# Attention reads and a mixture of experts on one core: x transposed by transfers inside SBUF, weights converted to fp16 on their way in

## The chip, the core and the metric

The kernel runs on one core of a Trainium2 chip. The metric is the device time of one execution in microseconds (us); less is better. Five engines work side by side, each through its own instruction queue and in the order in which the kernel recorded its instructions: TensorE (PE, matrix products; its weight loads are listed as PEld), VectorE (DVE), ScalarE (ACT), GpSimd (POOL) and SyncE (SP, which only issues transfers). Transfers (DMA) are issued from an engine's queue and run on 16 DMA engines beside it. TensorE and the transfers meet in SBUF; TensorE's products land in the eight banks of PSUM, from which DVE or ACT must copy ("evict") them.

## The reference

Stage one is attention between `x` (8 batches, 8 heads, 512 rows, 64 columns) and a small `state` (32 rows per head), both ways; stage two sends the 4352 resulting rows of 512 numbers through 8 experts, all of them, weighted by a routing matrix P that is normalised by rows and columns eight times (Sinkhorn).

```python
scores  = scale * x @ state.T;  a  = softmax(scores);   xread = a @ state
scores2 = scale * state @ x.T;  a2 = softmax(scores2);  sread = a2 @ x
x = concat([xread, sread], axis=2)          # rows of all heads side by side
P = exp(x @ w_gate - max)
for _ in range(8):                          # Sinkhorn
    P /= P.sum(1);  P /= P.sum(0);  P *= N / E
for e in range(E):
    out += P[:, e:e+1] * (relu(x @ w1[e]) @ w2[e])
```

`w1[e]` is 512 x 1024 and `w2[e]` is 1024 x 512, both fp32 in HBM: 4 MB per expert. `x` is 8 MB.

## The kernel before, in words

**Two stages of code.** Lines 353 to 858 build a list of operations `ops`, and `issue(ops)` (line 48) records them in an order of its own. The code calls this the plan of the first stage: attention for all batches, the gate and Sinkhorn, the whole of expert 0, and the first layer of expert 1 for two blocks. From line 884 on, a plain loop over experts 1 to 7 and nine blocks of rows (eight blocks of 512 rows, one per batch, and one of 256) records the second stage: `layer2` of one block interleaved with `layer1` of the next and `project` of the one after.

**The plan.** Each operation has engines with a busy time and a latency (the pairs in braces, in us), operations that it comes after, and buffers that it takes or uses. `issue` always records the operation that can start earliest by these numbers; among equals the lowest rank decides. Ranks are due times: `due_x(u)` (line 354) for half-batch `u` of attention, `due_e(bi)` (line 355) for block `bi` of expert 0, `due_1` (line 356) for expert 1. The plan only sets the order in each queue. On the chip every engine takes its queue strictly in that order and waits by semaphores.

**Attention, per batch `b`.** Two loads of 512 KB each (`load`, line 443, SP's queue, two buffers `x_st`) bring four heads each. A cast to fp16 into `x_nat` (line 448) runs on DVE and ACT for batch 0 and on POOL for batches 1 to 7, four instructions per half. Then `turn` (line 510) transposes `x_nat` on TensorE: four 128 x 128 transposes into one PSUM bank for each of four head pairs, 16 per batch, 128 in all. `keep` (line 515) evicts each bank into `xT` on DVE or ACT, 32 evictions in all. Each half-batch `q` then needs two head pairs of `xT`: scores `psA` and `psB` (lines 534 and 541), maxima, exponentials and sums on DVE and ACT, one normalisation `a` on POOL (`normA`, line 577), transposes back (lines 597 and 601), and `su_ps` (line 619), which reads `x_nat` again. The result is `aT` for the rows and `xsT` for the state side.

**Weights.** For experts 0 and 1, `weights_ops` (line 463) splits the 4 MB into eight loads of 512 KB on SP's queue into three staging buffers `wst`, each followed by a cast to fp16 on ACT or DVE (`cast`, line 478), to `w1h` and `w2h`. For experts 2 to 7, `load_w` (line 159) is a generator that the main loop advances now and then (`step`, line 875): eight loads on SP's queue (lines 170 and 175), each cast two turns later by ACT (line 181), and then eight subtractions on DVE (line 196) that build `T` from `w2h`. `w1h` and `w2h` have two buffers each, so expert `e+1` is loaded while `e` runs.

**Expert work on TensorE.** V products from `w1h` (`v_ps`, line 722, and line 237 in the second stage), first layer `hps` (line 746; line 252), second layer `yps` (line 781) for expert 0, and in the second stage seven products per block with a trick that needs sums on DVE (line 298; sums in lines 277 to 280). DVE adds the weighted result into `acc` (line 312). Experts 1 to 7 need P from Sinkhorn before their first addition; Sinkhorn (lines 669 to 703) runs as one chain between DVE and TensorE, whose matmul is `csb_ps` (line 701), and starts when the last gate product is there.

Of the kernel before, what the change touches and what calls it, by code (L numbers as in the profile page):

```python
# [87 lines left out]
def kernel(  # L88
# [64 lines left out]

    mwst = ctx.enter_context(tc.tile_pool(name="moe_wst", bufs=3))
    mw = ctx.enter_context(tc.tile_pool(name="moe_w", bufs=2))
# [3 lines left out]
    def load_w(e, engines):  # L159
# [3 lines left out]
        w16[e] = (w1h, w2h)  # L163
        casts = []
        n = NKC + NFB // 2
        for k in range(n + 2):
            if k < n:
                if k < NKC:
                    st = mwst.tile([128, F], FP32, name="w1st", tag="wst")
                    nc.sync.dma_start(out=st, in_=w1r[e, :, k, :])  # L170
                    casts.append((w1h[:, k, :], st))
                else:
                    g = k - NKC
                    st = mwst.tile([128, 2, Dm], FP32, name="w2st", tag="wst")
                    nc.sync.dma_start(out=st, in_=w2r[e, :, ds(g * 2, 2), :])
                    casts.append((w2h[:, ds(g * 2, 2), :], st))
            if k >= 2:
                dst, src = casts[k - 2]
                eng = engines[(k - 2) % len(engines)]
                if eng is nc.scalar:  # L180
                    nc.scalar.copy(out=dst, in_=src)  # L181
                else:
                    eng.tensor_copy(out=dst, in_=src)
            yield
# [19 lines left out]
    actx = ExitStack()  # L204
    axs = actx.enter_context(tc.tile_pool(name="attn_xs", bufs=2))
    axp = actx.enter_context(tc.tile_pool(name="attn_x", bufs=3))
# [146 lines left out]
    ops = []  # L353
    due_x = lambda u: 10.0 + 5.54 * u
    due_e = lambda bi: 25.1 + 13.7 * bi
    due_1 = 150.0
    rings = {"bank": Ring(8)}
# [28 lines left out]
    def dma(rank, kb, emit, after=(), takes=()):  # L386
        return op(rank, {"DMA": (kb / 330.0, kb / 330.0 + 2.2)}, lambda _: emit(), after, takes)


# [46 lines left out]

    xn = [slot(axp, 3, [128, NSC, H, D], FP16, "x_nat") for _ in range(B)]
    x_ready = []
    for b in range(B):
        for g in range(2):  # L440
            st = slot(axs, 2, [128, H // 2, NSC * D], FP32, "x_st")

            def load(b=b, g=g, st=st):
                nc.sync.dma_start(
                    out=st.tile,
                    in_=x[b, ds(g * 4, 4), :, :].rearrange("h (p sc) d -> p h (sc d)", sc=NSC))

            def cast(eng, b=b, g=g, st=st):
                src = st.tile.rearrange("p h (sc d) -> p sc h d", sc=NSC)
                for sc in range(NSC):  # L450
                    copy(eng, xn[b].tile[:, sc, ds(g * 4, 4), :], src[:, sc])

            d = dma((0 if b < 1 else due_x(2 * b - 2), b, 0), 512, load, takes=[st])
            on = {"DVE": (0.90, 1.10), "ACT": (1.35, 1.50)} if b == 0 else {"POOL": (1.65, 1.80)}
            x_ready.append(op((0, 3) if b == 0 else (due_x(2 * b - 2),), on, cast, [d] + x_ready[2 * b:],
                              [xn[b]] if g == 0 else [], [st] + ([xn[b]] if g else [])))
# [5 lines left out]

    def weights_ops(e, rank, on):
        w1 = slot(mw, 2, [128, NKC, F], FP16, "w1h")
        w2 = slot(mw, 2, [128, NFB, Dm], FP16, "w2h")
        wslots[e] = (w1, w2)
        for k in range(NKC + NFB // 2):
            first = k < NKC
            st = slot(mwst, 3, [128, F], FP32, "wst")

            def load(k=k, st=st):
                if k < NKC:
                    nc.sync.dma_start(out=st.tile, in_=w1r[e, :, k, :])
                else:
                    nc.sync.dma_start(out=st.tile.rearrange("p (a b) -> p a b", a=2),
                                      in_=w2r[e, :, ds((k - NKC) * 2, 2), :])

            def cast(eng, k=k, st=st):
                if k < NKC:
                    copy(eng, w1.tile[:, k, :], st.tile)  # L480
                else:
                    copy(eng, w2.tile[:, ds((k - NKC) * 2, 2), :],
                         st.tile.rearrange("p (a b) -> p a b", a=2))

            d = dma(rank + (k,), 512, load, [w_ready.get((e, k - 1))] if k == 1 else [], [st])
            takes = [w1] if k == 0 else [w2] if k == NKC else []
            before = [w_ready[e, 0]] if 0 < k < NKC else [w_ready[e, NKC]] if k > NKC else []
            w_ready[e, k] = op(rank + (k,), on, cast, [d] + before, takes, [st])

    def w1_ready(e):  # L490
        return [w_ready[e, k] for k in range(NKC)]

    def w2_ready(e):
        return [w_ready[e, k] for k in range(NKC, NKC + NFB // 2)]

    weights_ops(0, (3.0, 4), {"ACT": (0.95, 1.10), "DVE": (0.75, 0.95)})
    weights_ops(1, (due_1 - 30.0, 0), {"ACT": (0.95, 1.10), "DVE": (0.75, 0.95)})


# [4 lines left out]
    for b in range(B):  # L504
        xT = slot(axt, 2, [128, NP, S], FP16, "xT")
        xt_ready = {}
        for hp in range(NP):
            ps = psum([128, S], FP16, "xT_ps")

            def turn(_, b=b, hp=hp, ps=ps):  # L510
                for sc in range(NSC):
                    nc.tensor.transpose(ps.tile[:, ds(sc * 128, 128)],
                                        xn[b].tile[:, sc, ds(2 * hp, 2), :], identh)

            def keep(eng, hp=hp, ps=ps, xT=xT):
# [5 lines left out]
                              [t] + ([xt_ready[0]] if hp else []),  # L521
                              [] if hp else [xT], [ps] + ([xT] if hp else []))
        for q in range(NQ):
            r = lambda n, b=b, q=q: (due_x(2 * b + q) + 0.1 * 5.54 * n,)
            psA = psum([128, NSC, 4, Ns], FP32, "psA")
# [93 lines left out]
            def read(_, b=b, q=q, ETs=ETs, su=su):  # L619
                for par in range(2):  # L620
                    for sc in range(NSC):
                        nc.tensor.matmul(su.tile[:, par].rearrange("p i n -> p (i n)"),
                                         xn[b].tile[:, sc, ds(2 * (2 * q + par), 2), :],
                                         ETs.tile[:, sc, ds(par * 64, 64)],
# [129 lines left out]
    for bi in range(len(blocks)):  # L754
# [6 lines left out]
        for fb in range(NFB):  # L761
# [8 lines left out]

            t = op((due_e(bi) + 0.05 * 13.7 * fb,), {"PE": (0.44, 0.62)}, mul, deps, [ps], held)
            h_ready.append(op((due_e(bi) + 0.05 * 13.7 * fb,), EVICT32, act, [t], [h], [ps]))
            hT.append(h)
        for tk in range(tn // 128):
            yps = psum([128, Dm], FP32, "yps")
            last = None
            for half in range(2):
                def mul(_, tk=tk, half=half, yps=yps, hT=hT):
                    w2h = wslots[0][1].tile
                    for fb in range(half * NJ, half * NJ + NJ):  # L780
# [3 lines left out]
                fbs = range(half * NJ, half * NJ + NJ)  # L784
                last = op((due_e(bi) + 13.7 * (0.4 + 0.075 * (2 * tk + half)),), {"PE": (0.87, 1.04)}, mul,
                          [h_ready[fb] for fb in fbs] + w2_ready(0)[2 * half:2 * half + 2] + [last],
                          [] if half else [yps], [hT[fb] for fb in fbs] + ([yps] if half else []))
# [3 lines left out]

            op((due_e(bi) + 13.7 * (0.4 + 0.075 * (2 * tk + 1)),), EVICT32, keep, [last], [], [yps])

# [141 lines left out]
```

## Time and profile before

| what | value |
|---|---|
| median of 3 runs | 794.11 us (793.38 to 795.03) |
| the profiled execution | 794.67 us |
| its span, first to last instruction | 792.9 us |
| mean granted TensorE clock | 0.995 of full |
| busy: PE, DVE, ACT, POOL | 764.5, 648.8, 566.7, 39.5 us |
| bytes read from HBM, written | 42.48 MB, 8.91 MB |
| last `csb_ps` of Sinkhorn, end of its chain | 161.89 us, about 164.2 us |
| first product of the second stage's loop (line 298) | 165.46 us |

How to read it: a busy engine is one with an instruction under way. Matmuls overlap each other in the pipeline, so TensorE's busy time says whether it idles, not how fast it works; what one instruction costs is read from the distance between starts. A "group" gathers instructions of one line, engine and shape, with the mean duration of one and the idle time of the engine ahead of them. A "wait" says which engine stood still for which producer. The timeline merges equal instructions that follow each other: start, time from the first start to the last end, count.

### The profile page before, as it was taken

The numbers are of one execution on the slowest core, as the hardware profiler recorded it, in microseconds if no ns is written. First come the engines' busy times: TensorE is split into PE (matmuls) and PEld (weight loads), VectorE is DVE, ScalarE is ACT, GpSimd is POOL, SyncE is SP. The second block draws the span as 40 slices with busy tenths as digits, with TensorE's granted clock in tenths as the row PEclk, the third lists the DMA queues.
The fourth block names the chain that finished last, engine by engine and source line by source line (L and its number), as shares of the span: only waits on it lengthen the run. The fifth ranks groups of instructions, "written<-read, shape, count | busy, mean of one in ns | idle before, by whom it ended". The sixth has DMA issues, their size and how long they took to land.

```text
span 792.9 us, 16564 instructions
## 1 busy us (share of the span) xinstructions
PE 764.5 (96%) x6593; PEld 514.2 (65%) x6593; DVE 648.8 (82%) x1603; ACT 566.7 (71%) x1072; POOL 39.5 (5%) x80
## 2 busy tenths in 40 slices
PE   4899999989999999999999999999999999999996
PEld 3455554556667666766667666766667766767675
DVE  7898877787898888978788888978788888978885
ACT  5787776568977688577866688578866688576662
POOL 1543210000000000000000000000000000000000
PEclk9999999999999999999999999999999999999999
DMA  8874000002400033001410033001400030002233
GB/s 280 288 253 138 1 2 1 1 1 64 125 28 1 1 104 111 1 2 54 129 33 2 1 107 107 1 2 54 133 28 2 1 107 28 1 24 97 95 107 134
DMA packets 29535, 52.46 MB, mean 66 GB/s; under 512 B 4625, under 2 KB 12817, under 8 KB 29457
## 3 DMA queue, kind: packets, MB, share of 16 engines
q1 hardware_dynamic: 28368, 51.14, 20.3%
q8 instruction: 51, 0.84, 0.4%
q10 hardware_dynamic: 1088, 0.26, 0.2%
q14 instruction: 28, 0.22, 0.1%
HBM read 42.48 MB, written 8.91 MB: 65 GB/s over the span
## 4 chain that ended last, share of the span: by engine, by line
PE 63%; DVE 4%; ACT 2%; issue 0%; DVEq 0%
PE hps L252 22%; PE Bseed L298 16%; PE E L298 11%; PE A L298 10%; PE v_ps L237 3%; DVE acc L312 2%; ACT Hm L271 2%; DVE sm L277 1%; ACT w2h L181 1%; DVE sm L280 0%; DVE Hm L278 0%; DVE T L196 0%; DVE sm L279 0%; ACT w1h L181 0%; DVE acc L320 0%
## 5 line engine op out<-in xcount | busy, mean ns | idle before, releaser
L271 ACT ACTIVATE Hm<-hps 128x512 f16<-128x512 f32 (+1 forms) x488 | 262.3, 575 | 149.8 <-PE hps L252 138.9
L298 PEld LDWEIGHTS <-Hm 128*128 128x128 f16 x1904 | 185.4, 98 | 74.4 <-issue 3.9
L252 PE MATMUL hps<-aT,V 128*128 128x512 f16 x864 | 230.5, 379 | 0.0
L312 DVE SCALAR_TENSOR_TENSOR acc<-Bseed,Pmat,acc 128x256 f32<-128x256 f32 x357 | 156.9, 479 | 57.1 <-PE Bseed L298 53.6
L298 PEld LDWEIGHTS <-sm 128*128 128x128 f16 x1428 | 134.4, 98 | 54.9 <-DVE sm L277 24.4
L298 PE MATMUL Bseed<-T,Hm 128*128 128x256 f16 x952 | 124.5, 273 | 2.7 <-DVE acc L312 2.5
L298 PE MATMUL A<-w2h,Hm 128*128 128x256 f16 x952 | 126.1, 273 | 0.5
L252 PEld LDWEIGHTS <-V 128*128 128x128 f16 x864 | 84.5, 98 | 44.4
L241 ACT CAST V<-v_ps 128x512 f16<-128x512 f32 x216 | 111.0, 608 | 0.0
L312 DVE SCALAR_TENSOR_TENSOR acc<-E,Pmat,acc 128x256 f32<-128x256 f32 x238 | 104.4, 478 | 5.4 <-PE E L298 1.0
L277 DVE TENSOR_TENSOR sm<-Hm 128x512 f16<-128x512 f16 (+1 forms) x122 | 49.9, 409 | 21.6 <-ACT Hm L271 20.8
L298 PE MATMUL E<-T,sm 128*128 128x256 f16 x476 | 64.4, 274 | 0.7
L781 PE MATMUL yps<-w2h,hT 128*128 128x512 f16 x272 | 64.6, 379 | 0.0
L312 DVE SCALAR_TENSOR_TENSOR acc<-A,Pmat,acc 128x256 f32<-128x256 f32 x119 | 52.4, 479 | 15.0 <-PE A L298 14.9
L298 PE MATMUL Bseed<-T,sm 128*128 128x256 f16 x476 | 62.3, 272 | 2.3 <-ACT Bseed L323 2.3
L298 PE MATMUL E<-w2h,sm 128*128 128x256 f16 x476 | 62.3, 273 | 0.0
L278 DVE TENSOR_TENSOR Hm<-Hm 128x512 f16<-128x512 f16 (+1 forms) x122 | 50.0, 410 | 4.2
L280 DVE TENSOR_TENSOR sm<-Hm,sm 128x512 f16<-128x512 f16 (+1 forms) x122 | 50.0, 410 | 4.2
L279 DVE TENSOR_TENSOR sm<-sm,Hm 128x512 f16<-128x512 f16 (+1 forms) x122 | 49.1, 403 | 0.0
L323 ACT COPY Bseed<-A 128x512 f32<-128x512 f32 (+1 forms) x63 | 34.7, 552 | 18.7 <-PE A L298 15.6
L781 PEld LDWEIGHTS <-hT 128*128 128x128 f16 x272 | 24.8, 98 | 27.5 <-issue 2.6
L746 PE MATMUL hps<-aT,V 128*128 128x512 f16 x160 | 41.1, 389 | 0.4
(114 smaller groups left out, 626.1 us busy)
## 6 DMA issues: line engine op xcount, KB each, us to landing
w1st<-in_moe_w_dram SPq DMA_DIRECT2D x24, 512.0 KB, 3.6
w2st<-in_moe_w_dram SPq DMA_DIRECT2D x24, 512.0 KB, 3.6
x_st<-in_x_dram SPq DMA_DIRECT2D x16, 512.0 KB, 5.1
wst<-in_moe_w_dram SPq DMA_DIRECT2D x16, 512.0 KB, 6.1
out_dram<-acc SPq DMA_DIRECT2D x32, 256.0 KB, 3.1
out_dram<-acc SPq DMA_DIRECT2D x8, 64.0 KB, 1.7
st_st<-in_state_dram ACTq DMA_DIRECT2D x4, 64.0 KB, 3.2
st_st<-in_state_dram SPq DMA_DIRECT2D x4, 64.0 KB, 3.0
```

The costliest lines, as they stand in the source:

```text
L241: nc.scalar.copy(out=V[:, q, cols], in_=ps[q])
L252: nc.tensor.matmul(out, lhs, rhs, start=(k == 0), stop=(k == len(terms) - 1))
L271: nc.scalar.activation(out=Hm[:, i, j, :tn], in_=hps[:, :tn], func=AF.Relu)
L277: nc.vector.tensor_add(s1, a21, a22)
L278: nc.vector.tensor_sub(a21, a11, a21)
L279: nc.vector.tensor_sub(s2, s1, a11)
L280: nc.vector.tensor_sub(s4, a12, s2)
L298: nc.tensor.matmul(dst[:, c], lhs(j, c), rhs[:, j], start=first and c == 0 and j == 0, stop=(j == NJ - 1), skip_group_check=True)
L312: nc.vector.scalar_tensor_tensor(out=dst, in0=src[:, c], scalar=p[:, k], in1=dst, op0=ALU.mult, op1=ALU.add)
L323: nc.scalar.copy(out=Bb[:, :nk], in_=A[:, :nk])
L746: nc.tensor.matmul(ps.tile[:, :tn], lhs, rhs, start=(k == 0), stop=(k == len(terms) - 1))
L781: nc.tensor.matmul(yps.tile, hT[fb].tile[:, ds(tk * 128, 128)], w2h[:, fb, :], start=(fb == 0), stop=(fb == NFB - 1))
```

## The change

Three things change together; the arithmetic stays.

1. For batches 1 to 7 the 16 TensorE transposes and their four evictions per batch go. In their place two transfers per batch, issued from SP's queue, read half of `x_nat` ([128, 1024] fp16, 256 KB) and write it transposed, in blocks of 128 x 128, into `xT`, SBUF to SBUF. Batch 0 stays on TensorE. `x_nat` gets another layout for it, `x_st` gets three buffers instead of two.
2. All weights are loaded by GpSimd's queue in transfers of 1 MB of fp32, four per expert, which convert to fp16 on the way and write `w1h` and `w2h` directly. The staging buffers and all weight casts on ACT and DVE go. In `load_w` three empty turns follow the four transfers, so the subtractions for `T` come at turn 8 rather than at turn 11.
3. The due times change: `due_x` 10.0 + 5.77u, `due_e` 27.5 + 14.7bi, `due_1` 100, and expert 1's weights get rank 50 instead of 120. The plan is made anew with them, so the order in every queue of the first stage differs.

```diff
-        for k in range(n + 2):
...
+        for k in range(2):
+            nc.gpsimd.dma_start(out=w1h[:, ds(2 * k, 2)], in_=w1r[e, :, ds(2 * k, 2), :])
+            yield
+        for k in range(2):
+            nc.gpsimd.dma_start(out=w2h[:, ds(k * NJ, NJ)], in_=w2r[e, :, ds(k * NJ, NJ), :])
+            yield
+        for _ in range(3):
             yield
...
-    axs = actx.enter_context(tc.tile_pool(name="attn_xs", bufs=2))
+    axs = actx.enter_context(tc.tile_pool(name="attn_xs", bufs=3))
...
-    due_x = lambda u: 10.0 + 5.54 * u
-    due_e = lambda bi: 25.1 + 13.7 * bi
-    due_1 = 150.0
+    due_x = lambda u: 10.0 + 5.77 * u
+    due_e = lambda bi: 27.5 + 14.7 * bi
+    due_1 = 100.0
...
+    def dma16(rank, kb, emit, after=(), takes=(), uses=()):
+        asked = op(rank, {"POOL": (1.0, 1.0)}, lambda _: emit(), after, takes, uses)
+        return op(rank, {"DMA": (kb / 330.0, kb / 330.0 + 2.2)}, lambda _: None, [asked])
...
-    xn = [slot(axp, 3, [128, NSC, H, D], FP16, "x_nat") for _ in range(B)]
+    xn = [slot(axp, 3, [128, NP, NSC, 128], FP16, "x_nat") for _ in range(B)]
...
+            w_ready[e, k] = dma16(rank + (k,), 1024, load, [w_ready[e, k - 1]] if k % 2 else [],
+                                  [] if k % 2 else [w2 if k else w1], [w2 if k > 1 else w1] if k % 2 else [])
...
-    weights_ops(1, (due_1 - 30.0, 0), {"ACT": (0.95, 1.10), "DVE": (0.75, 0.95)})
+    weights_ops(1, (due_1 - 50.0, 0))
...
-        for hp in range(NP):
+        for hp in range(NP if b < 1 else 0):
...
+        for g in range(2 if b >= 1 else 0):
+            def turn(_, b=b, g=g, xT=xT):
+                nc.sync.dma_start_transpose(
+                    out=xT.tile[:, ds(2 * g, 2)].rearrange("p a (s t) -> p (a s) t", t=128),
+                    in_=xn[b].tile[:, ds(2 * g, 2)].rearrange("p a s c -> p (a s c)"))
+
+            t = op((due_x(2 * b + g) - 2.0, 0), {"SP": (1.6, 4.0)}, turn,
+                   [x_ready[2 * b + g]] + ([xt_ready[0]] if g else []), [] if g else [xT],
+                   [xn[b]] + ([xT] if g else []))
+            xt_ready[2 * g] = xt_ready[2 * g + 1] = t
```

## The prediction

> **What bounds the kernel now.** I read the busy time by stretches first, then the waits, then the timeline of TensorE.
>
> ```profile
> core 0: us, PE busy (x) PEld busy (x) DVE busy (x) ACT busy (x) POOL busy (x), PEclk, DMA share, GB/s
> 0.00:60.00 60.00, 45.56 (x466) 26.17 (x467) 49.55 (x117) 42.45 (x83) 23.68 (x55) 0.97 0.82 272
> 60.00:120.00 60.00, 59.68 (x577) 32.13 (x576) 49.18 (x117) 44.37 (x101) 15.82 (x25) 1.00 0.14 45
> 300.00:700.00 400.00, 399.29 (x3433) 282.29 (x3431) 330.25 (x822) 293.67 (x544) 0.00 (x0) 1.00 0.15 44
> ```
>
> Three stages. From 300 us on TensorE never idles (399.3 of 400), with ACT and DVE a fifth to a quarter idle. From 60 to 120 us the same. Only up to 60 us does TensorE stand idle, 14.4 us, while the transfers are 82% busy and DVE 83%.
>
> ```profile
> ACT Hm L271 <- PE hps L252: 138.9, 209, 1.9
> ```
>
> The longest wait of the run is ACT's for TensorE: in the second stage ACT has time to spare.
>
> ```profile
> 89.30 0.61 PE L512 MATMUL xT_ps<-identh,x_nat 128*128 128x128 f16 x8
> 89.74 1.03 PE L781 MATMUL yps<-w2h,hT 128*128 128x512 f16 x4
> ```
>
> Eight transposes of x hold TensorE from 89.30 to 89.74, where the next product starts: 0.44 us, 55 ns each (the group's mean of 241 ns counts overlap).
>
> ```profile
> 161.89 0.39 PE L701 MATMUL csb_ps<-cpart,ones 128*128 128x8 f32 x2
> 165.03 0.59 PE L871 MATMUL Bseed<-aT,identh 128*128 128x512 f16 x2 [1.01 <-ACT Hm L382]
> 165.46 1.04 PE L298 MATMUL A<-w2h,Hm 128*128 128x256 f16 x8
> ```
>
> The first stage ends for TensorE and for Sinkhorn together, at about 164 us; its last gate product was at 125.17 us, so Sinkhorn takes 39 us.
>
> **Part 1, transposes leave TensorE.** 7 batches x 16 x 55 ns = 6.2 us less on TensorE, which is full from 60 us to the end of the stage, so I count all of it. It shows at both ends: pricing the recorded matmuls of both orders by their distances in the trace (hps and yps 216 ns, psA 40, psB 166, v_ps 44, transposes 55, su_ps 30), the work ahead of the last gate falls from 100.7 to 93.4 us and the whole stage's from 136.7 to 130.5. Sinkhorn can thus start 7 us sooner, and TensorE runs dry 6 us sooner.
>
> The evictions go too:
>
> ```profile
> L376 ACT COPY xT<-xT_ps x18: 583/592/626, 12.8 to 110.7; 128x512 f16<-128x512 f16 x18
> L378 DVE COPY xT<-xT_ps x14: 361/415/425, 9.5 to 102.7; 128x512 f16<-128x512 f16 x14
> ```
>
> 18 x 0.59 + 14 x 0.41 = 16.1 us, less batch 0's four (2.0): 14 us of DVE and ACT, at nothing after 60 us, since TensorE covers them.
>
> What it adds: 14 transfers of 256 KB on SP's queue. The trace has none that transposes. Bounds from its packets: rows of 256 bytes (the state loads; 1088 packets on q10 took 0.2% of 16 engines' 792.9 us, 23 ns each) give 1024 x 23 / 16 = 1.5 us. Pieces of 32 bytes (the gate weights, 9 ns each in the packet records) give 8192 x 9 / 16 = 4.6 us. Between issue and landing some 2 to 3 us come on top (64 KB land after 1.7 us when stored, 3.0 to 3.2 when loaded).
>
> ```profile
> x_st<-in_x_dram SPq DMA_DIRECT2D x16, 512.0 KB, 5.1
> out_dram<-acc SPq DMA_DIRECT2D x32, 256.0 KB, 3.1
> wst<-in_moe_w_dram SPq DMA_DIRECT2D x16, 512.0 KB, 6.1
> ```
>
> So 3.1 us (same bytes, no transposing) to 4.6 + 3 = 7.6 us to landing; I take 4.5, near the rows of equal or double size, and keep both. Is that hidden? In the new order the first scores of batch 1 stand after 7.3 us of TensorE work, of batch 2 after 14.5, of batch 3 after 24.7, and two buffers `xT` let the transfers run one batch ahead; a batch lasts about 11 us. Two transfers at 3 to 4.6 us fit. Two that hold the stream more than 6.5 us each do not (rival B).
>
> SP's queue is in order: a transfer that waits for POOL's cast holds the x loads behind it. `x_st` has three buffers, so after the transfer of batch 1's first half three loads leave at once. Since weights no longer take turns in that queue, I cost this at nothing; if the cover goes, each batch arrives later by one wait, and rival B's sum holds.
>
> The timeline has 55 ns of TensorE's time for a 128 x 128 transpose among others; no row has one by transfer. The Trainium skill, "VectorE: DVE Perf Modes", section "The three transpose paths", speaks against the change: it lists 390 ns on TensorE and 1309 ns by transfer for one block. If that second figure were a price per block, a transfer of eight blocks would take 10.5 us (an estimate from that page) and rival B's sum would give 850 us.
>
> **Part 2, converting weight loads.** For experts 0 and 1, 16 casts (9 on ACT, 9.45 us; 7 on DVE, 6.27 us) go, all before 60 us, where DVE and ACT limit. In the second stage 48 casts of 1.04 us go from ACT: nothing from 300 us on, since ACT waits there anyway; between 165 and 260 us TensorE idles 4.8 of 95 us (90.23 busy), partly behind ACT and DVE: I take 1 us, bounds 0 and 3.
>
> Added: eight issues on POOL in the first stage. SP takes 0.37 to 0.5 us for an issue, POOL's normalisation 1.1 us; I take 1.0 each. In the new order five stand at the head of POOL's queue and end at about 1.8 + 5 = 7 us, long before the first normalisation.
>
> ```profile
> 15.14 1.43 POOL L378 CAST x_nat<-x_st 128x256 f16<-128x256 f32 x4 [13.33 <-DMA x_st<-in_x_dram]
> 16.53 1.10 POOL L578 TENSOR_TENSOR a<-eA,rA 128x512 f16<-128x512 f32 x1
> ```
>
> They matter only above (16 - 2) / 5 = 2.8 us each. What they do early is compete: 5 MB of weights are asked for by 7 us, beside x. In the trace 512 KB land every 1.3 us when the queue is full (weights at 11.04, 12.30, 13.63 us), 1 MB in 2.6 us. x of batch 0 landed at 7.89 and 9.46 us; with half the rate its second half lands 2.6 us later, and if 1 KB packets of x alternate with 4 KB packets of weights, about 9 us later. Against that stand three w1h casts ahead of the first hps at 24.74 us, two of ACT (1.05 each) and one or two of DVE (0.69), some 3 us, and a first transposing transfer that must wait behind a normalisation on POOL (about 1 us). Bounds -4 to +6 us, taken as 0.
>
> Conversion itself: as fast as plain loads (3 MB in 8 us) or as slow as 256-byte packets (178 GB/s, 17 us). w1h is whole at 15 to 25 us; the first v_ps now starts at 19.44 us. In the second stage 4 MB per expert, 628 us for seven experts, is little either way, and `T`'s subtractions, three turns earlier, come over 20 us after the request.
>
> **Part 3, due times.** Attention gets a little further ahead of expert 0, expert 1 moves ahead of expert 0's last blocks: the same work in another order, counted in the sums above, 0.
>
> **Sum, against the profiled execution of 794.67 us:** -6.2 (TensorE) - 1 (ACT, 165 to 260 us) + 0.7 (first waits on transposing transfers, of the bound 0 to 3) = -6.5, so 788.2. The median of the runs is 0.6 lower than the profiled execution; I give 788.
>
> **Rivals.**
>
> A. *The start gives it back.* x's first megabyte shares the transfers with 5 MB of weights, attention of batch 0 starts up to 6 us late, and TensorE, which has nothing else then, shifts as a whole. For: 82% busy transfers, TensorE idle 14 us up to 60 us. Against: fewer casts in just that stretch. 794.67 - 7.2 + 6 = 793.5.
>
> B. *Transposing transfers become the bound (slower).* First half ready at about 20 us; 14 in a row at t each; from the last scores (111.62 us) to the stage's end (164.2) the trace takes 52.6 us. End = 20 + 14t + 52.6: at 6.5 us it equals today's; at 7 it is 170.6 (801 us), at 8 184.6 (815 us). For: no row shows such a transfer, and one stream in SP's queue takes all 14. Against: the packets bound it at 4.6 us.
>
> C. *POOL is the bound (slower).* Issues above 2.8 us each delay normalisation and casts; at 4 us the first normalisation slips 6 us, and three later issues hold casts 3 us longer each, half of it hidden: 788.2 + 6 + 4.5 = 798.7. For: POOL serves one queue in order. Against: SP's issues take a tenth of that.
>
> D. *The start gains too:* DVE and ACT are relieved of 22 of 92 us before 60 us and TensorE's idle time shrinks by 4 us more: 783.
>
> That the change does not do what it says is excluded: the new order has 16 transposes of x on TensorE, not 128, and no weight cast.
>
> **How the numbers follow.** Forecast 0.50 (786 to 791), A 0.20, B 0.18, C 0.07, D 0.05. A difference under 0.2%, 1.6 us, cannot be told from none. Faster: 0.50 + 0.05 + a third of A (0.07) = 0.62. Same: 0.12 of A. Slower: 0.18 + 0.07 + 0.01 = 0.26. The range runs from D's far side, 782, to B at just over 7 us, 803; about 0.04 lies below and 0.16 above.
>
> **What would show it.** Right: the last csb_ps near 155 us, TensorE full from 50 us on, transposing transfers landing 4 to 5 us after issue, no psA that waits for xT after batch 1. Wrong: psA waiting for a transposing transfer in every batch (B), x of batch 0 landing after 12 us (A), POOL idle gaps at its issues (C), or a change beyond 300 us, where I expect none.

## The result, and the profile after

| | before | after |
|---|---|---|
| median | 793.64 us (793.22 to 795.03) | 795.16 us (793.96 to 798.05) |
| ratio, 95% interval | | 1.0023 [1.0014, 1.0031] |
| span of the profiled execution | 792.9 us | 793.9 us |
| first product `psA` of TensorE | 11.02 us | 23.83 us |
| first product of the second stage's loop | 165.46 us | 172.62 us |
| from there to the last product | 621.5 us | 615.3 us |

The change made the kernel slower by 0.23%, where I had forecast 0.8% faster. The table already says where: the loop over experts begins 7.2 us later and lasts 6.15 us less. The sum, 1.0 us, is the difference of the spans. Two large effects nearly cancel.

The same stretches as before the change, in the changed kernel:

```profile
core 0: us, PE busy (x) PEld busy (x) DVE busy (x) ACT busy (x) POOL busy (x), PEclk, DMA share, GB/s
0.00:60.00 60.00, 31.89 (x307) 17.86 (x308) 33.49 (x79) 22.77 (x52) 22.75 (x51) 0.97 0.91 187
60.00:120.00 60.00, 59.30 (x557) 30.04 (x556) 51.47 (x123) 44.76 (x97) 20.86 (x37) 1.00 0.46 95
300.00:700.00 400.00, 399.62 (x3457) 283.14 (x3455) 331.52 (x827) 265.98 (x510) 11.63 (x16) 1.00 0.13 22
```

Up to 60 us TensorE is busy 31.9 us, where it was 45.6. ACT and DVE, relieved of their casts, stand idle with it (22.8 and 33.5 us busy, before 42.5 and 49.6): with less of their own work TensorE is busy less, not more, so they do not limit this stretch. The transfer engines are 91% busy at 187 GB/s in place of 272; that counts bytes as written, and a converting load writes half of what it reads.

The end of the first stage on TensorE's timeline, and the longest wait of the run:

```profile
171.53 0.39 PE L690 MATMUL csb_ps<-cpart,ones 128*128 128x8 f32 x2 [0.60 <-DVE cpart L677]
172.18 0.61 PE L860 MATMUL Bseed<-aT,identh 128*128 128x512 f16 x2 [0.26 <-DVE crec L683]
172.62 1.04 PE L284 MATMUL A<-w2h,Hm 128*128 128x256 f16 x8
```

```profile
ACT Hm L257 <- PE hps L238: 166.7, 245, 1.9
```

The last `csb_ps` comes at 171.5 us; I had named 155 as the mark of my forecast. ACT waits for TensorE even longer than before, so the second stage is still TensorE's.

The issues (KB as written, median us to landing) and, for the tile `xT`, the transposing transfers:

```profile
w1h<-in_moe_w_dram POOLq DMA_DIRECT2D x16, 512.0 KB, 7.0
x_st<-in_x_dram SPq DMA_DIRECT2D x16, 512.0 KB, 6.4
xT<-x_nat SPq DMA_TRANSPOSE x14, 4.4
```

```profile
L504 SPq DMA_TRANSPOSE xT<-x_nat x14: 1232/1418/4128, 32.2 to 94.5; - x14
DMA to landing us min/median/max: 3.1/4.4/12.1
```

A transposing transfer lands after 4.4 us in the median; I had taken 4.5. Its spread, 3.1 to 12.1 us, is the new thing.

Now the start. By stretches of 20 us, the kernel before and then the changed one:

```profile
0.00:20.00 20.00, 9.94 (x113) 7.15 (x113) 13.97 (x35) 10.11 (x20) 3.63 (x13) 1.00 0.87 279
20.00:40.00 20.00, 16.68 (x180) 8.90 (x173) 16.50 (x40) 15.70 (x31) 10.29 (x23) 0.91 0.86 289
40.00:60.00 20.00, 18.94 (x184) 10.12 (x183) 19.08 (x43) 16.64 (x35) 9.75 (x19) 1.00 0.73 249
```

```profile
0.00:20.00 20.00, 3.39 (x24) 2.52 (x25) 7.02 (x16) 2.85 (x4) 4.84 (x13) 1.00 1.01 196
20.00:40.00 20.00, 12.47 (x155) 7.23 (x155) 12.47 (x30) 9.38 (x23) 5.60 (x11) 1.00 0.64 140
40.00:60.00 20.00, 16.03 (x130) 8.11 (x129) 14.00 (x34) 10.55 (x26) 12.31 (x28) 0.91 1.08 226
```

TensorE's timeline in the changed kernel says what the start waits for, and the two loads of batch 0 (tile `x_st`, issues up to 5 us; first before, then after) say why:

```profile
15.82 1.32 PE L491 MATMUL xT_ps<-identh,x_nat 128*128 128x128 f16 x8 [3.90 <-DVE x_nat L364]
22.88 1.02 PE L419 MATMUL G_ps<-wgh,bdT 128*64 128x8 f16 x32 [5.74 <-DVE wgh L399]
23.83 0.61 PE L526 MATMUL psA<-bdT,xT 128*128 128x64 f16 x8
```

```profile
DMA to landing us min/median/max: 4.4/4.9/5.5
```

```profile
DMA to landing us min/median/max: 11.9/14.0/16.1
```

x of batch 0 lands at 15.45 and 20.04 us (before 7.89 and 9.46), and the 16 KB of gate weights, issued behind it, at 22.62 (before 9.64). Their product `G_ps` stands ahead of `psA` in TensorE's queue, so the first scores start at 23.83. Five converting transfers, 5 MB, were asked for between 1.76 and 5.5 us, the first three ahead of x (issued at 3.52 and 3.98 us), all five ahead of the gate weights (5.17 us).

**TensorE's half-clock spells.** One thing blurs a comparison of starts. In eight of the fifteen profiled executions TensorE's granted clock falls to half for 3.41 us once or twice in the first 70 us (before: once at 24.5 us, which is the 0.91 above; after: once at 56.4; in e3 the two follow on each other). In 10 us of the kernel before, with the clock in the third column from the end, it reads

```profile
20.00:30.00 10.00, 8.07 (x92) 4.37 (x84) 8.89 (x21) 8.37 (x18) 3.94 (x9) 0.83 0.94 299
```

and (1 - 0.83) x 10 = 1.7 us, the most that a spell can cost. It varies between executions of one kernel. Below, "corrected" is the start of the loop less 1.71 us for each spell in that profile: a bound, since a spell before a wait costs less. The mean clock of every execution says how much less: a spell lowers it by 0.0022, so an execution at 0.999 or more has none. In the kernel before, the 30 such executions have a median of 793.9 us, and 11 at 0.996 or less 793.6: its spells cost nothing that shows. In the changed kernel ten at 0.999 have 794.8 us, six at 0.996 or less 797.4. So the changed kernel is slower without spells too, and "corrected" suits it better than the kernel before. A start of that kernel without a spell is in e5, whose first stage is the same: 164.5 us.

### The profile page after: what moved, and what is told of

It is laid out like the page before. It is cut to its first block, busy times and chain, and to the rows that moved or that the text cites. A ratio compares the mean times of both kernels' runs of the same rounds, so it can differ in the third digit from the quotient of the medians.

```text
span 793.9 us, 16207 instructions
## 1 busy us (share of the span) xinstructions
PE 756.8 (95%) x6481; PEld 507.4 (64%) x6481; DVE 638.4 (80%) x1581; ACT 513.4 (65%) x1002; POOL 62.2 (8%) x112
## 3 DMA queue, kind: packets, MB, share of 16 engines
q0 software_dynamic: 12800, 16.78, 12.9%
## 4 chain that ended last, share of the span: by engine, by line
PE 66%; DVE 3%; ACT 1%; issue 0%
PE hps L238 23%; PE Bseed L284 17%; PE E L284 12%; PE A L284 11%; PE v_ps L223 3%; DVE acc L298 1%; DVE sm L263 1%; ACT Hm L257 1%; DVE Hm L264 0%; DVE sm L266 0%; DVE sm L265 0%; DVE T L182 0%; ACT Bseed L309 0%
## 5 line engine op out<-in xcount | busy, mean ns | idle before, releaser
L238 PE MATMUL hps<-aT,V 128*128 128x512 f16 x864 | 230.6, 379 | 0.0
L284 PE MATMUL A<-w2h,Hm 128*128 128x256 f16 x952 | 124.5, 273 | 0.0
L164 POOL DMA_DIRECT2D w1h<-in_moe_w_dram x12 | 8.5, 714 | 452.8 <-PE hps L238 406.9
```

The lines of the kernel that those rows point to most:

```text
L238: nc.tensor.matmul(out, lhs, rhs, start=(k == 0), stop=(k == len(terms) - 1))
L284: nc.tensor.matmul(dst[:, c], lhs(j, c), rhs[:, j], start=first and c == 0 and j == 0, stop=(j == NJ - 1), skip_group_check=True)
```

## The experiments

All thirteen in one table: median and ratio to the kernel before, first `psA`, first `psA` of batch 1, first product of the loop, the same corrected, and the time from there to the last product.

| run | median us | ratio, 95% interval | psA | psA of batch 1 | loop | corrected | loop lasts |
|---|---|---|---|---|---|---|---|
| before | 793.6 | 1 | 11.0 | 23.5 | 165.5 | 163.8 | 621.5 |
| after | 795.2 | 1.0023 [1.0014, 1.0031] | 23.8 | 37.9 | 172.6 | 170.9 | 615.3 |
| e1 | 795.3 | 1.0024 [1.0014, 1.0035] | 11.0 | 22.6 | 166.1 | 162.7 | 621.5 |
| e2 | 802.4 | 1.0112 [1.0097, 1.0127] | 24.1 | 36.7 | 176.9 | 176.9 | 617.0 |
| e3 | 795.6 | 1.0022 [1.0011, 1.0033] | 19.2 | 35.3 | 172.3 | 168.9 | 615.3 |
| e4 | 799.1 | 1.0071 [1.0056, 1.0085] | 10.9 | 27.6 | 174.7 | 173.0 | 615.3 |
| e5 | 789.7 | 0.9949 [0.9937, 0.9961] | 10.9 | 23.1 | 164.5 | 164.5 | 617.0 |
| e6 | 787.0 | 0.9919 [0.9906, 0.9932] | 11.0 | 23.2 | 162.3 | 162.3 | 617.0 |
| e7 | 790.0 | 0.9951 [0.9938, 0.9964] | 19.0 | 32.9 | 167.0 | 165.3 | 615.3 |
| e8 | 791.0 | 0.9962 [0.9950, 0.9975] | 16.0 | 30.1 | 165.8 | 165.8 | 615.3 |
| e9 | 790.6 | 0.9956 [0.9942, 0.9969] | 11.0 | 23.2 | 165.5 | 162.1 | 617.0 |
| e10 | 789.4 | 0.9939 [0.9916, 0.9961] | 11.2 | 23.8 | 160.8 | 160.8 | 617.2 |
| e11 | 793.2 | 0.9995 [0.9985, 1.0004] | 10.9 | 21.8 | 164.6 | 164.6 | 619.8 |
| e12 | 795.0 | 1.0022 [1.0012, 1.0033] | 25.0 | 37.2 | 174.6 | 172.9 | 615.3 |
| e13 | 788.2 | 0.9928 [0.9916, 0.9940] | 19.7 | 31.9 | 165.4 | 165.4 | 615.3 |

**e1: the transposing transfers alone** (kernel before; weights, due times and buffers of x as before).

```diff
-    xn = [slot(axp, 3, [128, NSC, H, D], FP16, "x_nat") for _ in range(B)]
+    xn = [slot(axp, 3, [128, NP, NSC, 128], FP16, "x_nat") for _ in range(B)]
...
-        for hp in range(NP):
+        for hp in range(NP if b < 1 else 0):
...
+        for g in range(2 if b >= 1 else 0):
...
+                nc.sync.dma_start_transpose(
```

> Transposes of batches 1 to 7 by transfer, everything else (weights, plan numbers) as before. Theory S (start: the weights asked for at once on GpSimd's queue hold back x of batch 0, 15.45 and 20.04 us instead of 7.89 and 9.46; the 12.8 us by which the first psA comes later pass one to one to the end of the first stage, while the transposes save their 6.2 us): first psA at 11 us, first product of the second stage's loop at 159 to 160 us instead of 165.5, second stage 621.5 us as before, time 787 to 788 us, ratio about 0.992. Theory T (the transposing transfers are what makes the first stage longer, by psA waiting for xT): the loop starts at 165 us or later, time 793 us or more, ratio at least 1.0.

The start is as before and TensorE waits for transposing transfers only 1.8 us in all, yet the loop begins no sooner and the time is 1.8 us longer: the figures that theory T named, without its wait. Of the 6.2 us nothing is left in the medians; the 1.0 us of the corrected column is a bound, and e1's executions with fewer spells are no faster (795.7 us at a clock of 0.998, 795.0 at 0.991). In stretches:

```profile
20.00:40.00 20.00, 16.20 (x140) 7.64 (x138) 17.11 (x36) 13.88 (x30) 8.37 (x19) 0.83 1.11 307
40.00:60.00 20.00, 16.02 (x149) 8.34 (x150) 14.45 (x36) 13.51 (x26) 10.27 (x23) 1.00 1.07 312
```

The transfer engines are full (1.11 and 1.07; before 0.86 and 0.73). Each transposing transfer adds about 1.8 us of all 16 (24.6 us of busy time in all over 14), x lands 3 to 5 us later for batches 3 to 6, and TensorE idles where it transposed. Neither theory had this. I read it as work saved without room for the transfers that replace it. It is not shown apart from SyncE's order: the loads of x for batches 3 to 6 are also asked for up to 4.5 us later, behind transposing transfers in the same queue.

**e2: the converting weights alone** (kernel before, with the changed `weights_ops` and `load_w`; all transposes on TensorE and the due times of before; x keeps the three buffers and the layout of the changed kernel).

```diff
-        for k in range(NKC + NFB // 2):
...
+        for k in range(NKC):
+            def load(k=k):
+                if k < 2:
+                    nc.gpsimd.dma_start(out=w1.tile[:, ds(2 * k, 2)], in_=w1r[e, :, ds(2 * k, 2), :])
```

> Weights converted on GpSimd's queue, all batches transposed on TensorE, plan numbers of before. Theory S: first psA at about 24 us, loop starts at 165.5 + 12.8 = 178 us, second stage 615 us (as in the changed kernel), time about 799 us, ratio 1.007. Theory T: the loop starts at 165 us, time 787 us, ratio 0.992.

The loop begins 12.4 us later than in e5, the same start without a spell, and 13.1 us later than before, corrected: nearly all of the 13.1 us by which the first `psA` comes later. The medians say the same: 8.9 us slower than the kernel before, where e5, with the same 617.0 us behind, is 4.1 faster, so 13.0 us. 4.5 us come back in the second stage. Together e1 and e2 do not add up: with the weights changed, the transposing transfers bring 176.85 - 170.91 = 5.9 us, nearly all of the 6.2 (the due times differ too; e11 has them alone). As I read it (the profiles do not prove it), TensorE then has a backlog and the transfer engines idle stretches (0.64 busy between 20 and 40 us).

**e3: gate weights first** (changed kernel).

```diff
-    wgd = dma((0, 2), 16, lambda: nc.sync.dma_start(
+    wgd = dma((0, 0), 16, lambda: nc.sync.dma_start(
```

> The changed kernel with the 16 KB load of the gate weights ahead of the state and x loads in SP's queue, nothing else on purpose. Theory S with the small load as a part of it (the G products stand ahead of the first psA in TensorE's queue and waited for that load until 22.88 us): first half-batch's psA at 17 to 18 us, second half's at 22 instead of 26.2, time 4 us less, about 790 us, ratio 0.995. Theory T: no difference to the changed kernel, 795 us, ratio 1.002.

`psA` starts 4.7 us sooner, but its second half, which waits for x, at 23.4 in place of 26.2, and the median is that of the changed kernel: theory T's figures, not the 4 us that I expected. The gate weights were the first gate only; x stood right behind it. Spells hide a smaller gain: ten of the twelve executions have a clock of 0.996 or less, and the two at 0.998 and 0.999 take 793.0 us, 1.8 less than the changed kernel without spells.

**e4: weights only behind x of batch 0** (e3, and the converting transfers come after a small read of x's second half on GpSimd).

```diff
+            if b == 0 and g == 1:
+                x_in.append(op((0, 3), {"POOL": (0.2, 0.3)}, lambda _, st=st: nc.gpsimd.tensor_copy(
+                    out=mark, in_=st.tile[:, 0, 0:1]), [d], [], [st]))
...
-            w_ready[e, k] = dma16(rank + (k,), 1024, load, [w_ready[e, k - 1]] if k % 2 else [],
+            w_ready[e, k] = dma16(rank + (k,), 1024, load, x_in + ([w_ready[e, k - 1]] if k % 2 else []),
```

> The changed kernel with the gate weights' load first and GpSimd asking for the first weights only when x of batch 0 has landed (it copies one number of it first). Theory S: x of batch 0 at 8 and 9.5 us, first psA at about 11 us, first v_ps at 20 to 23 us, loop starts at 160 to 161 us, second stage 615 us, time 782 us, ratio 0.985. Theory T: the loop starts at 168 us or later, time 790 us or more.

The start is that of before, 10.9 us, and the kernel is slower still. TensorE's waits:

```profile
PE psA L531 <- DMA xT<-x_nat: 11.4, 2, 9.5
```

The first two transposing transfers of batch 1 went out at 12.65 and 15.02 us, among 6 MB of weights that GpSimd asked for between 9.6 and 21.7 us, and landed after 14.9 and 19.2 us:

```profile
L509 SPq DMA_TRANSPOSE xT<-x_nat x2: 1649/7254/12858, 12.7 to 15.0; - x2
DMA to landing us min/median/max: 14.9/17.0/19.2
```

SyncE held the second for 12.9 us at its issue. So the weights delay whatever needs the transfer engines next: x of batch 0, or batch 1's x and its transposition. The figures are those of theory T, but it is the weights that make the transposing transfers late; both of my theories were too narrow.

**e5: converting weights in the second stage only** (kernel before; only `load_w` changes).

```diff
-        casts = []
...
+        for k in range(2):
+            nc.gpsimd.dma_start(out=w1h[:, ds(2 * k, 2)], in_=w1r[e, :, ds(2 * k, 2), :])
+            yield
+        for k in range(2):
+            nc.gpsimd.dma_start(out=w2h[:, ds(k * NJ, NJ)], in_=w2r[e, :, ds(k * NJ, NJ), :])
+            yield
```

> The kernel before, with one edit: the weights of experts 2 to 7 come as fp16 by converting transfers on GpSimd's queue, four of 1 MB each, in place of eight loads on SyncE's queue, eight casts on ScalarE and VectorE and their fp32 buffers. The first stage is the one of before, word for word, the transposes on TensorE. Theory P (the whole change is a gain of 4 to 6 us behind the first product of the loop over experts, given back ahead of it): first psA at 11.0 us and the first product of the loop at 165.5 us as before, the second stage near 617 us as in the run with the weights alone (88.6 to 88.8 us an expert in place of 88.9 to 91.5), so 789 us, ratio 0.994. Rival Q (the shorter second stage is the late start's doing: an expert 1 whose weights and output state are further along): the second stage stays at 621 us, 793.5 us, ratio 1.000.

Theory P: 789.7 us. The loop lasts 617.0 us. Its first pass, expert 1, takes 88.8 us in place of 91.5. That stretch, before, in e5:

```profile
165.00:260.00 95.00, 90.23 (x788) 63.10 (x788) 80.66 (x203) 72.59 (x134) 0.00 (x0) 1.00 0.15 46
```

```profile
165.00:260.00 95.00, 92.60 (x810) 65.36 (x808) 81.73 (x206) 67.11 (x129) 2.91 (x4) 1.00 0.15 24
```

**e6: e5 with transposing transfers for batches 5 to 7** (as e1, from another batch on).

```diff
+        for hp in range(NP if b < 5 else 0):
...
+        for g in range(2 if b >= 5 else 0):
```

> The kernel of the run before this one, with x of batches 5 to 7 transposed by transfers within SBUF; those are issued after 60 us, where the transfer engines of the kernel before are busy 0.4 or less. Theory C (the transposing transfers give back what they save because they share the transfer engines with x and the weights of the first 75 us): six of them land in 3.2 to 4.5 us, no score product waits for one, TensorE is rid of 3 x 0.89 = 2.7 us, and the first product of the loop comes 1.5 to 2.7 us sooner than in the run before. Rival W (the first stage isn't set by TensorE's work there, or the issue on SyncE holds the x loads): the same within 0.5 us.

787.0 us, the best of all by its median. The six transfers landed in 3.2 to 5.8 us, none was waited for, and the loop begins 2.2 us sooner for 2.65 us less of TensorE's work. Where the transfer engines have room (0.41 between 60 and 80 us), the transposing transfers pay as I had reckoned.

**e7: weights of expert 1 later** (changed kernel).

```diff
-            w_ready[e, k] = dma16(rank + (k,), 1024, load, [w_ready[e, k - 1]] if k % 2 else [],
+            w_ready[e, k] = dma16(rank + (k,), 1024, load, (x_ready[-1:] if e else []) + ([w_ready[e, k - 1]] if k % 2 else []),
```

> The changed kernel, with GpSimd asking for the weights of expert 1 only behind its last cast of x (in the changed kernel at 45 to 75 us, among the transfers of x and the transposing ones; here near 90 us). Theory C (contention of small packets with the converting transfers): the transposing transfers of batches 2 to 5 land in about 4 us in place of 9.6 to 12.1, and the first product of the loop comes 1 to 4 us sooner than 172.6. Rival (the delay is all made before 45 us, where nothing changes): 172.6 within 0.5 us, ratio 1.002 as the changed kernel's. In both the weights of expert 1 are there by 110 us, and the second stage stays at 615.3 us.

5.6 us sooner, 790.0 us: one added dependency turns the change into a gain. My text had the place half wrong. The plan of the changed kernel had asked for the first megabyte of expert 1 already at 4.79 us and the second at 29.98, so e7 also takes 1 MB from the start: `psA` comes 4.8 us sooner, that of batch 1 4.9 us, so this run does not tell the start from the middle. In the middle the transposing transfers of 44 to 55 us land after 3.1 to 6.2 us; in the changed kernel those of 46 to 55 us after 5.9 to 9.6:

```profile
L504 SPq DMA_TRANSPOSE xT<-x_nat x4: 1233/2176/2427, 44.3 to 54.5; - x4
DMA to landing us min/median/max: 3.1/5.5/6.2
```

**e8: narrow packets** (changed kernel, experts 0 and 1).

```diff
+                for c in range(0, F if k < 2 else Dm, 256):
+                    cs = ds(c, 256)
+                    if k < 2:
+                        nc.gpsimd.dma_start(out=w1.tile[:, ds(2 * k, 2), cs],
+                                            in_=w1r[e, :, ds(2 * k, 2), cs])
```

> The changed kernel, with each converting transfer of the first stage (experts 0 and 1) split into strips of 256 columns: w1 in 8 transfers, w2 in 4 of the same bytes, so that a packet carries 1 KB of fp32 in place of 4 or 2 KB. If the transfer engines take turns packet by packet among their queues (theory C), x and the transposing transfers get a larger share: x(0,1) lands near 13 to 16 us in place of 20.0, transposing transfers beside weights in 5 to 8 us in place of 9.6 to 12.1, while the weights of expert 0 land later and GpSimd spends some 10 us more on issues. If instead the order of the requests or the bandwidth of HBM sets when x lands (rival), x(0,1) stays near 20 us. The time: between 793 and 798 us, as the later weights and the sooner x pull against each other.

x of batch 0 lands at 10.43 and 13.19 us in place of 15.45 and 20.04. Two things changed at once: the packets are smaller, and GpSimd, at 0.72 us for each 256 KB, has asked for 0.75 MB of weights when x is asked for, not for 3 MB. That packets take turns the traces show by themselves. While x and weights are both under way, in the changed kernel (8 to 12 us) and in e8 (10 to 13 us), the weights' queue (q0) and the one of x (q1) get nearly the same number of packets (packets, MB as written, share of the 16 engines' time; in e8 450 of q1's are the small pieces of the gate weights):

```profile
q0 software_dynamic: 485, 0.50, 75.0%
q1 hardware_dynamic: 450, 0.45, 40.7%
```

```profile
q0 software_dynamic: 774, 0.38, 92.6%
q1 hardware_dynamic: 776, 0.32, 57.5%
```

With equal turns, the 485 larger packets took 75% of the engines' time and the 450 of x 41%. So the share that x gets depends on the size of the packets it takes turns with; how much of its earlier landing in e8 is the order of asking is open. The other half failed: transposing transfers beside weights still took 7.4 to 11.6 us. The transfer engines are fuller (1.30 between 40 and 60 us), and the loop begins 5.1 us sooner, corrected; I had expected no gain (793 to 798 us).

**e9: e6 with batches 3 to 7.**

```diff
-        for hp in range(NP if b < 5 else 0):
+        for hp in range(NP if b < 3 else 0):
...
-        for g in range(2 if b >= 5 else 0):
+        for g in range(2 if b >= 3 else 0):
```

> The kernel of e6 with x of batches 3 to 7 turned by transfers in place of 5 to 7, so that four more transposing transfers stand between 35 and 55 us, where the transfer engines of that kernel are busy 0.8 to 0.9 and eight loads of expert 1's weights stand too. Theory C (a transposing transfer pays only where the transfer engines have room): the four cost about 1.8 us of all 16 engines each, x of batches 4 to 6 lands 2 to 5 us later than in e6, and the 1.8 us of TensorE saved are given back: first product of the loop between 162 and 165, 787 to 790 us. Rival (each batch turned by transfers is worth its 0.89 us of TensorE wherever it stands): 160.5 us and 785.2 us.

3.6 us slower than e6 and the loop 3.2 us later, with 1.8 us less work on TensorE. This profile has two half-clock spells where that of e6 has none; corrected, the loop begins at the same time, 162.1 against 162.3. But spells do not make the difference: e9's two executions at a clock of 0.999 take 790.7 and 791.2 us, e6's one 787.0. So the 1.8 us was given back and some 3.6 us more lost, which speaks for C.

**e10: e6 with expert 1 by late converting transfers.**

```diff
-    weights_ops(1, (due_1 - 30.0, 0), {"ACT": (0.95, 1.10), "DVE": (0.75, 0.95)})
...
+        w_ready[1, k] = dma16((due_1 - 30.0, 0, k), 1024, load, x_ready[-1:] + ([w_ready[1, k - 1]] if k % 2 else []),
```

> The kernel of e6 with the weights of expert 1 as four converting transfers of 1 MB, asked for behind the last cast of x on GpSimd (near 80 us), in place of eight loads at 24 to 52 us and eight casts on ScalarE and VectorE. Theory C (what the first stage loses up to 60 us is the transfer engines shared by x and these weights): x of batches 2 to 6 lands 2 to 5 us sooner, TensorE is idle 1 to 3 us less between 20 and 60 us, and the first product of the loop comes at 159.5 to 161.5 in place of 162.3; the last transposing transfers land in 5 to 9 us beside the weights, which costs up to 1 us. 784 to 786 us. Rival (TensorE's idle time there is the length of each batch's own chain, not the landing of x): 162.3 within 0.5 us, 787 us.

```profile
20.00:40.00 20.00, 18.08 (x186) 9.85 (x179) 17.57 (x40) 15.62 (x35) 11.17 (x26) 1.00 0.65 201
40.00:60.00 20.00, 19.99 (x189) 10.68 (x188) 15.81 (x40) 15.20 (x34) 8.15 (x17) 1.00 0.62 158
```

In the profile TensorE is busy 38.1 of 40 us (e6: 35.7, the transfer engines at 0.91 and 0.81) and the loop begins at 160.8, as theory C had it; the casts of expert 1 went as well, so the transfers' room is not alone in this. The last three transposing transfers took 7.9 to 15.0 us beside the late weights, where I had named 5 to 9. The executions scatter from 785.8 to 792.6 us, and the profiled one, without a spell, is the fastest. The other five have lower clocks (0.994 to 0.996 against 0.998), which can account for 1.6 to 3.2 us each, not for the 3.6 to 6.9 us that four of them are behind. The median is no better than e6's.

**e11: the due times alone** (kernel before; also the two other places where 5.54 and 13.7 stand).

```diff
-    due_x = lambda u: 10.0 + 5.54 * u
-    due_e = lambda bi: 25.1 + 13.7 * bi
-    due_1 = 150.0
+    due_x = lambda u: 10.0 + 5.77 * u
+    due_e = lambda bi: 27.5 + 14.7 * bi
+    due_1 = 100.0
...
-    weights_ops(1, (due_1 - 30.0, 0), {"ACT": (0.95, 1.10), "DVE": (0.75, 0.95)})
+    weights_ops(1, (due_1 - 50.0, 0), {"ACT": (0.95, 1.10), "DVE": (0.75, 0.95)})
```

> The kernel before with only the planner's due times of the changed kernel (a step of 5.77 in place of 5.54 for x, 14.7 in place of 13.7 for expert 0, expert 1 due at 100 in place of 150) and its three buffers for x in place of two where room allows them; transposes, weights and casts as before. My working gave the due times nothing: 793.5 us within 1.5. Rival (the due times are what moved the order of the first stage, and so the late start of the loop): first product of the loop later than 168 us, 796 us or more.

793.2 us: the plan's numbers aren't the cause of the late loop, which begins as in e5 (164.6 and 164.5 us). But the loop lasts 619.8 us in place of 621.5: its first pass, expert 1, takes 89.9 us and not 91.5. The same 1.7 us lie between the runs with converting weights and the due times of before (617.0) and those with the changed ones (615.3). So a part of the second stage's gain is the due times'. (The buffers of x stayed at two.)

**e12: batch 1 back on TensorE** (changed kernel).

```diff
-        for hp in range(NP if b < 1 else 0):
+        for hp in range(NP if b < 2 else 0):
...
-        for g in range(2 if b >= 1 else 0):
+        for g in range(2 if b >= 2 else 0):
```

> The changed kernel with batch 1 turned on TensorE too (transposing transfers for batches 2 to 7 only), weights and plan numbers as changed. In the changed kernel the first transposing transfer stands ahead of four loads of x in SyncE's queue and waits there from 6 to 32 us for a cast on GpSimd, and the transfer engines are busy only 0.33 between 20 and 30 us. Theory H (the held queue is a part of the late start of its own, beside the weights that go first): x(1,1) is asked for near 17 us in place of 33.7 and lands by 26, the transfer engines are busy 0.6 or more between 20 and 30 us, and the first product of the loop comes 2 to 5 us sooner than 172.6 although TensorE has 0.9 us more to do: 790 to 793 us. Rival (the late first product is the weights' going first alone, and x of batch 1 would wait for casts on GpSimd anyway): 172.6 to 173.5, 795 to 796 us. TensorE's half-clock spells (3.4 us each, none to two in the first 70 us) are subtracted on both sides at 1.7 us each before the two are compared.

x(1,1) did land at 26.8 us, and the transfer engines were busy 0.65 between 20 and 30 us, in place of 0.33. The loop begins no sooner, and the executions without a spell take 794.9 us against 794.8: theory H, with its 2 to 5 us, falls. GpSimd's timeline in the changed kernel shows a part of why:

```profile
28.88 1.15 POOL L567 TENSOR_TENSOR a<-eA,rA 128x512 f16<-128x512 f32 x1 [23.36 <-DVE rrec L558]
29.98 0.81 POOL L464 DMA_DIRECT2D w2h<-in_moe_w_dram  x1
30.79 1.43 POOL L364 CAST x_nat<-x_st 128x256 f16<-128x256 f32 x4
```

The casts of batch 1's first half stand behind batch 0's normalisation, which comes at the end of the chain that begins with the late `psA`. Those of the second half do come sooner in e12, at 35.3 us in place of 38.9; why the loop does not is open.

**e13: e12 and e7 together** (the two edits above in one kernel).

> The kernel of e12 with the weights of expert 1 asked for behind the last cast of x, as in e7. What it tells apart: if the held queue and the weights of expert 1 delay different stretches, their gains add: the first product of the loop near 172.6 - 5.6 - (2 to 5) = 162 to 165 us, and 785 to 788 us. If both only shorten the same wait, no better than e7: 167 us and 790 us.

165.4 us, as e7 corrected, and 788.2 us, between the two theories. The median is 1.8 us better than e7's, and a spell does not explain it: without one, e7 takes 789.5 and 790.0 us, this kernel 788.2 in the median of three. So once the weights of expert 1 are out of the way, freeing SyncE's queue is worth some 1.5 us. GpSimd's casts behind the second normalisation, in e7 and then here, show the wait that is gone:

```profile
33.78 3.00 POOL L364 CAST x_nat<-x_st 128x256 f16<-128x256 f32 x8 [4.41 <-DMA x_st<-in_x_dram]
```

```profile
30.02 2.79 POOL L364 CAST x_nat<-x_st 128x256 f16<-128x256 f32 x8
```

## Why the prediction was wrong, point by point

- **What bounds the kernel now.** I read "transfers 82% busy and DVE 83%" up to 60 us, and relieved DVE. The runs speak for the transfers: with some 22 us of casts and evictions gone, DVE and ACT simply idled more, and e1, which relieves them and loads the transfers, gains nothing.
- **Part 1, -6.2 us of TensorE.** The size of the work was right: 112 transposes fewer are recorded ahead of the loop, at 55 ns each. Counting all of it was only right where TensorE has a backlog (5.9 us of it from e2 to after; 2.2 of 2.65 in e6). Beside full transfers it isn't there (nothing in the medians of e1).
- **Landing of 4.5 us, hidden.** The median was right (4.4), the bound was not: 7.6 us was the upper end, and beside converting transfers up to 19.2 us were measured. The rows that I took came from a queue that has the engines to itself. Rival B, 14 transfers of over 6.5 us in a row, did not happen; e4 is near it for one batch.
- **SyncE's queue held behind a transposing transfer, at nothing.** It was held from 11.6 to 32.2 us (the load of x ahead of it took 5.4 us to issue). In e12 freeing it gains nothing, and why is open; in e13 it is worth some 1.5 us.
- **Part 2, "Bounds -4 to +6 us, taken as 0".** This is the step that failed. I had worked out that x's second half could come "about 9 us later" (it came 10.6 later), then set against it the relief of casts, which was worth nothing, and stopped at x. The first `psA` came 12.8 us later, since the gate weights land behind x and `G_ps` stands ahead of `psA`. And I looked for the delay to be absorbed, while TensorE never makes up for it: the loop begins 7.2 us later with 6.2 us less to do, so 13.3 us more of TensorE's time are lost ahead of it than before (both profiles have one spell). e2, which has this part alone, begins the loop 12.4 us later than e5.
- **Casts in the second stage, -1 us (0 to 3), none from 300 us on.** Mis-sized: e5, which has it alone, shows -4.5 us. 2.8 of them are in the first pass of the loop (165 to 257 us), inside the bounds, and 0.26 to 0.46 us in each of the next five passes, where I had expected none.
- **GpSimd's issues at 1.0 us.** 0.70 to 0.84 us; rival C did not happen.
- **Part 3, due times, at nothing.** Right ahead of the loop, wrong behind it: 1.7 us less in the first pass (e11). With the casts' 2.8 us this makes up the 4.45 us by which that pass is shorter in the changed kernel (91.54 to 87.09 us).
- **The sum.** Ahead of the loop the weights cost 13.1 us and the transposes saved 5.9 (both corrected), 7.2 us in all; behind its start 6.15 us were gained: +1.0 us, where I had -6.5. Rival A had the mechanism, with 6 us where 12.8 were due, and without the second stage's gain. (18 x 0.59 + 14 x 0.41 is 16.4, not 16.1, and rival D's sum gives 784, not 783; neither moves the forecast.) The time came out between my forecast and rival B for neither's reason.

What stays open: what decides how many half-clock spells an execution has; what else makes e10's executions scatter; and whether e1 lost its gain to full transfer engines or to the order in SyncE's queue.

## What to carry to other kernels

Transfer engines that are 82% busy have little room: before moving work onto them, add up what must land by when, and put what is wanted last at the end of the asking, not at the head of a queue that happens to be free. Taking the casts out of the weights' path was worth 4 us where transfers had room, and the same edit cost 13 us where 5 MB of weights that were needed later went ahead of or beside x and 16 KB of gate weights that everything waited for. Follow the late piece to the first instruction in each queue that needs it, however small it is.

## What the runs showed of the hardware

- **Small packets beside large ones.** A load of 512 KB of x in rows of 1 KB landed after 4.4 to 5.5 us at the head of the kernel before and 5.0 to 7.5 us among its staged loads, after 11.9 to 16.1 us beside converting transfers with rows of 4 and 2 KB, and after 7.1 to 9.4 us beside converting transfers with rows of 1 KB, of which less had been asked for (e8). The Trainium skill, "DMA: Bandwidth & Descriptors", section "Queues, rings and completion order", says that each engine takes turns among its queues packet by packet; the packet counts agree with it (485 and 450, 774 and 776), and so do the loads of x; the transposing transfers of e8 do not land sooner for it.
- **Transposing within SBUF.** 256 KB in eight blocks of 128 x 128 took 3.1 to 3.3 us from issue to landing with the engines free, 1.23 us of it SyncE's issue. The 1309 ns of the skill's "VectorE: DVE Perf Modes", section "The three transpose paths", are no price per block of such a transfer.
- **Converting loads took about as long as plain ones.** In the first 23 us 1 MB of fp32 arrived as fp16 every 2.6 to 4.1 us, with x landing among them (before: 512 KB every 1.3 us), and the issue took GpSimd 0.70 to 0.84 us.
- **Half-clock spells.** Each lasted 3.41 us (one of 6.83 in e3), at half the clock, and began from 0.3 us before to 2.0 us after the end of a stretch in which TensorE had idled 0.9 to 5.3 us; not each such stretch was followed by one. The Trainium skill, "TensorE: Matmul & The Clock Gate", section "Part 1: The HAM clock gate", gives a free-running window of 3413 ns; the length agrees, and so does that equal kernels differ in it. The same section has the clock fall after a whole idle window; here eight of the ten spells followed idle stretches of 0.9 to 2.2 us.
